# Attention with a mixture of experts: scaling and splitting v on GpSimd, and a softmax sum's constants by a two-tensor instruction

## The chip, the core and the metric

The kernel runs on one core of a Trainium2 chip. The metric is the time of one execution in device microseconds. TensorE (PE in the profile) does the matmuls, VectorE (DVE), ScalarE (ACT) and GpSimd (POOL) the element-wise work, and SyncE (SP) issues every DMA from one queue, in order. Each engine runs its own instructions in order and waits for others by semaphores.

## The reference, cut to what matters

```python
def _attn_ref(q, k, v, w1, b1, w2):          # q, k, v: 4 x 8 x 576 x 64
    scores = scale * np.matmul(q, k.transpose(0, 1, 3, 2))
    ...
    scores = scores + bias.transpose(2, 0, 1)[None, :, :, :]
    scores = scores - np.max(scores, axis=-1, keepdims=True)
    attn = np.exp(scores)
    attn = attn / (np.sum(attn, axis=-1, keepdims=True) + 1e-09)
    return np.matmul(attn, v).astype(np.float32)

def _moe_ref(x, w_gate, w1, w2):             # 2304 tokens, 8 experts
    P = np.exp(logits)
    ...
    for e in range(E):
        h = np.maximum(x @ w1[e], 0.0)
        ye = h @ w2[e]
        out += P[:, e:e + 1] * ye
```

The bias is a small network of the positions, the same in every batch. P is normalized by rows and columns eight times.

## The kernel before

All matmuls are done in float16. A float32 operand is scaled by a power of two and split into two float16 parts, hi (the rounded value) and lo (the rest), and products of the parts are summed. So a split is two instructions: one that scales and rounds, one that scales again and subtracts hi.

**The two parts of the program.** The first part, about 490 us long, is the attention, with the bias before it and the work of expert 0 mixed into it. The second part is experts 1 to 7. The change touches the first part alone.

**The attention.** There are 16 units: a batch and a pair of heads. Each unit has five steps: (gi 0, hh 0), (gi 0, hh 1), (gi 1, hh 0), (gi 1, hh 1) with two query tiles each, and gi 2 with one. Per unit, `u_load` fetches q and k, `u_cut` splits them into `qk` (ACT writes hi, DVE lo), and `u_trans` transposes `qk` on PE and has POOL copy rows of `qkT` between partitions. `u_vload` fetches v into `vnat`, of which there is one buffer; `u_v` splits it into `vs` with `asplit`: ACT writes `vs[:, 0]`, DVE `vs[:, 1]`. Three POOL copies (`pairs`) then arrange a third plane, `vs[:, 2]`, out of hi and lo. `vs` has two buffers (units 2 and 3 use room in `xb` instead). A tile of a step goes: scores on PE; `st_max` on DVE (a custom instruction, ISA in the listings, which adds the bias, writes `sb` and its extreme to `st`); `st_exp` on ACT, with the sums into `st`; `st_rcp` on DVE, two instructions on one or two columns of `st` (add 1e-9 and multiply by 2^-14, then the reciprocal); `st_hi` on ACT and `st_lo` on DVE, which write the split probabilities `ah` (one in three into room in `xc`); a DMA transpose of `ah` into `aT`; and two steps later `attend` on PE, `pv`<-`aT`,`vs`.

**Filling work.** When a batch is done, `e0_pieces` gives its matmuls through expert 0 to PE with the lowest priority. Their first layer is evacuated by `l1_out`: ACT into `ys`, then two POOL instructions, a cast and a subtraction, into `area`.

**The order of the work.** Everything is recorded as nodes of a `Plan` with an engine, an estimated cost (`Engine.cost`) and its dependencies, and `Plan.emit` puts all engines' instructions in order by list scheduling with these estimates. A node that changes engine or cost thus moves others too. All recorded instructions have the line of the recorder's call, L211, so rows are told apart by tiles.

The calls that bring v in come from the table of hooks, where step number 5u belongs to unit u:

```python
hook(f - 3, lambda u=u: [u_vload(u), u_v(u)])
...
hook(2, lambda: [b_scale(2), u_vload(0), u_v(0), u_load(3), u_cut(3), u_trans(3)])
```

Of the kernel before, what the change touches and what calls it, by code (L numbers as in the profile page):

```python
# [10 lines left out]
F32 = mybir.dt.float32  # L11
U32 = mybir.dt.uint32
AF = mybir.ActivationFunctionType
ALU = mybir.AluOpType
# [4 lines left out]
P = 128  # L19
# [8 lines left out]
EPS = 1e-9  # L28
T14 = 2.0**14
TM14 = 2.0**-14  # L30
# [7 lines left out]
MXP = 2  # L38
K_VEC = (1, 4, 7)
TM16 = 2.0**-16  # L40
TINY = 2.0**-100


# [228 lines left out]
def attention_sinkhorn_moe(ctx, tc, q, k, v, w1, b1, w2, wg, m1, m2, xm, xm4, xf, sel, out):  # L272
# [10 lines left out]
    nc = tc.nc  # L283
    plan = Plan()
    vec, act, pool, pe, sync = (
        Engine(plan, e, n)
        for e, n in ((nc.vector, "dve"), (nc.scalar, "act"), (nc.gpsimd, "pool"), (nc.tensor, "pe"), (nc.sync, "dma"))
    )

    consts = ctx.enter_context(tc.tile_pool(name="consts", bufs=1))  # L290
# [7 lines left out]
    def sm(shape):  # L298
        used[0] += shape[1]
        assert used[0] <= SMALL  # L300
        return sms[: shape[0], used[0] - shape[1] : used[0]]
# [5 lines left out]
    def bcast_max(psum_tile, mx, n, between=None):  # L307

        pt = psum_tile()
        pe.transpose(pt[:n, :P], mx, ident)  # L310
        col = sm([n, 1])
        vec.tensor_reduce(out=col, in_=pt[:n, :P], axis=AX.X, op=ALU.max)
        diag = sm([n, n])
        vec.tensor_scalar(out=diag, in0=ident[:n, :n], scalar1=col[:, 0:1], scalar2=None, op0=ALU.mult)
        if between is not None:
            between()
        pb = psum_tile()
        pe.matmul(pb[:, :n], ones[:n, :], diag, start=True, stop=True)
        res = sm([P, n])
        vec.tensor_copy(res, pb[:, :n])  # L320
        return res

    def pow2(mx, n, unit, clamp):

        p = sm([P, n])
        vec.tensor_single_scalar(out=p.bitcast(U32), in_=mx.bitcast(U32), scalar=0x7F800000, op=ALU.bitwise_and)
        u = sm([P, n])
        vec.tensor_scalar(out=u, in0=p, scalar1=clamp, scalar2=unit, op0=ALU.max, op1=ALU.mult)
        s = sm([P, n])
        vec.reciprocal(out=s, in_=u)  # L330
        return u, s

    def absmax(o, i):
        vec.tensor_reduce(out=o, in_=i, axis=AX.X, op=ALU.max, apply_absolute_value=True)
# [8 lines left out]
    def split(hi, lo, src, s):  # L343
        vec.tensor_scalar(out=hi, in0=src, scalar1=s, scalar2=None, op0=ALU.mult)
        vec.scalar_tensor_tensor(out=lo, in0=src, scalar=s, in1=hi, op0=ALU.mult, op1=ALU.subtract)

    def asplit(hi, lo, src, s):
        act.activation(hi, src, AF.Copy, scale=s)
        vec.scalar_tensor_tensor(out=lo, in0=src, scalar=s, in1=hi, op0=ALU.mult, op1=ALU.subtract)
# [15 lines left out]
    def xs(part, dt, pos, W):  # L365
        b, o = pos // 512, pos % 512
        return xv[b][:, part, dt, o : o + W]
# [47 lines left out]
    with ExitStack() as actx:  # L415
# [40 lines left out]

        make_identity(nc, ident)
        nc.gpsimd.memset(ones, 1.0)
        nc.vector.tensor_copy(id16, ident)


# [55 lines left out]
        absmax(mxb[:, 0:1], wb.rearrange("p a k -> p (a k)"))  # L517
        u_wb, s_wb = pow2(mxb[:, 0:1], 1, 2.0**-9, TINY)
        wbs = scon.tile([P, 2, 2, HID], F16, name="wbs")
# [4 lines left out]
        for kind in range(1, 4):  # L524
            vec.scalar_tensor_tensor(
                out=wr,
                in0=wbs[:, kind // 2, kind % 2, :],
                scalar=selt[:, kind : kind + 1],
                in1=wr,
                op0=ALU.mult,  # L530
                op1=ALU.add,
# [3 lines left out]
            out=wa.rearrange("p g (j k) -> p (g j) k", j=4),  # L535
            in0=wr.unsqueeze(1).broadcast_to([P, 16, HID]),
            in1=selt[:, 8:24].unsqueeze(2).broadcast_to([P, 16, HID]),
            op=ALU.mult,
# [89 lines left out]
        def bias_step(between=()):  # L628
# [22 lines left out]
        absmax(mxb[:, 1:2], w2b)  # L651
        u_w2, s_w2 = pow2(mxb[:, 1:2], 1, TM14, TINY)

        w1r = scon.tile([P, 2], F32, name="w1r")
        vec.tensor_scalar(
            out=w1r, in0=pw[:, H : H + 2], scalar1=s_wb[:, 0:1], scalar2=2.0**-11, op0=ALU.mult, op1=ALU.mult
# [5 lines left out]
            out=w2m,  # L662
            in0=w2r.unsqueeze(2).broadcast_to([P, H, 4]),
            in1=selt[:, 4:8].unsqueeze(1).broadcast_to([P, H, 4]),
            op=ALU.mult,
# [65 lines left out]
        def pairs(o, i):  # L731
            pool.tensor_copy(o.bitcast(U32), i.bitcast(U32))

        def u_v(u):
            if u >= len(units):
                return
            st = U[u]
            if u in (2, 3):
                o = 30 * D * (u - 2)
                vs = xb[:, o : o + 30 * D].rearrange("p (w h c d) -> p w h c d", w=3, h=2, c=5)  # L740
            else:
                vs = uni.tile([P, 3, 2, 5, D], F16, name="vs", tag="vs")
            vf = lambda t: t.rearrange("p h c d -> p (h c) d")
            asplit(vf(vs[:, 0]), vf(vs[:, 1]), vf(st.pop("vn")), vbox[1])

            pairs(vs[64:128, 2], vs[0:64, 0])
            pairs(vs[0:64, 2, :, 1:5], vs[64:128, 0, :, 0:4])
            pairs(vs[0:64, 2, :, 0], vs[0:64, 0, :, 4])
            st["vs"] = vs
# [59 lines left out]
        with plan.urgent():  # L809
# [6 lines left out]
            out=c8, in0=u_qk[:, 0:1], scalar=0.125, in1=u_qk[:, 1:2], op0=ALU.mult, op1=ALU.mult  # L816
# [7 lines left out]
            out=g, in0=g0, scalar=s_qk[:, 0:1], in1=s_qk[:, 1:2], op0=ALU.mult, op1=ALU.mult  # L824
# [11 lines left out]
        mv8, vbox = sm([P, 8]), []  # L836
# [6 lines left out]
        def v_scale():  # L843
            mv = sm([P, 1])
            vec.tensor_reduce(out=mv, in_=mv8, axis=AX.X, op=ALU.max)
            with plan.urgent():
                u_, s_ = pow2(bcast_max(ps_small, mv, 1), 1, TM14, TINY)
            vbox.extend((u_[:, 0:1], s_[:, 0:1]))
# [101 lines left out]

        def st_rcp(s):
            st, n = s["st"], len(s["ts"])
            vec.tensor_scalar(
                out=st[:, 3, :n], in0=st[:, 2, :n], scalar1=EPS, scalar2=TM14, op0=ALU.add, op1=ALU.mult
            )
            vec.reciprocal(out=st[:, 3, :n], in_=st[:, 3, :n])

# [29 lines left out]
        def attend(u, gi, ss):  # L987
# [25 lines left out]
            def fin():  # L1013
                hi, lo = xs(0, hp, pos, W), xs(1, hp, pos, W)
                act.activation(hi, ps[:, :W], AF.Copy, scale=TM16)
                vec.scalar_tensor_tensor(
                    out=lo, in0=ps[:, :W], scalar=TM16, in1=hi, op0=ALU.mult, op1=ALU.subtract
                )
# [29 lines left out]
        def w_scale(which):  # L1048
# [7 lines left out]
            with plan.urgent():  # L1056
                u_, s_ = pow2(bcast_max(ps_small, m, n), n, TM14, TINY)
            wsc[which] = (u_[:, 0:1], s_[:, 0:1])
# [88 lines left out]
        for n in range(NS + LAG + 1):  # L1147
            while xevac:
                xevac.pop(0)()
            if 0 < n <= NS:  # L1150
                st_rcp(steps[n - 1])
# [15 lines left out]
            if 0 < n <= NS:  # L1167
                s = steps[n - 1]
                st_hi(s)
                st_lo(s)  # L1170
                u, gi, hh = s["key"]
# [24 lines left out]
        vec, act, pool, pe, sync = nc.vector, nc.scalar, nc.gpsimd, nc.tensor, nc.sync  # L1196
# [289 lines left out]
    def w_max(e, w):  # L1486
# [20 lines left out]
        def scale(mx):  # L1507
# [3 lines left out]
            vec.tensor_single_scalar(out=p.bitcast(U32), in_=m.bitcast(U32), scalar=0x7F800000, op=ALU.bitwise_and)  # L1511
            vec.tensor_scalar(out=u, in0=p, scalar1=TINY, scalar2=TM12, op0=ALU.max, op1=ALU.mult)
            vec.reciprocal(out=s, in_=u)
# [487 lines left out]
```

## Time and profile before

| | us |
|---|---|
| median of 3 runs | 1741.65 (1737.5 to 1742.94) |
| the profiled execution | 1741.8 |
| its span, first to last instruction | 1740.0 |
| PE busy in the span | 1666.5 (96%) |
| DVE busy | 1437.2 (83%) |
| ACT busy | 1057.8 (61%) |
| POOL busy | 149.3 (9%) |

The span is what the trace shows; 1.8 us of the execution's own time lie outside of it. Busy shares are averages over the two parts, which have different limits, so the prediction reads the first part by itself.

### The profile page before, as it was taken

To read this page: it belongs to the slowest core of one execution; us is meant where nothing else is said; L and a number is where in the kernel's file an instruction comes from. 1 tells how busy PE (TensorE), PEld (TensorE's weight loads), DVE (VectorE), ACT (ScalarE), POOL (GpSimd) and SP (SyncE) were. 2 spreads that over 40 slices of the span, in tenths; PEclk is the share of its full clock that TensorE was granted. 3 is DMA by queue.
4 is the path that set the end of the run, shared out by engine and by line. 5 is a ranking of instruction groups with operands and counts; after the bars stand their busy time and mean duration, and the time that the engine had idled before them with its cause. 6 is when DMAs were issued, how large, how long until landed. Compare 5 with 4: busy or idle time off the path is not lost.

```text
span 1740.0 us, 40362 instructions
## 1 busy us (share of the span) xinstructions
PE 1666.5 (96%) x16596; PEld 1367.8 (79%) x16596; DVE 1437.2 (83%) x2595; ACT 1057.8 (61%) x1879; POOL 149.3 (9%) x191
## 2 busy tenths in 40 slices
PE   7887897999999999999999999999999999999998
PEld 4554564656585888888988898889888888888887
DVE  7998999889769999687878887988788878876666
ACT  7887888888857555456455545555555644443443
POOL 0102231323212300000000000000000000000000
PEclk9988898999999999999999999999999999999999
DMA  7869999999875446644664555456544743462321
GB/s 256 257 174 233 186 205 216 212 213 213 177 239 200 158 161 239 232 150 143 217 231 170 176 190 209 176 178 238 203 165 159 279 157 131 183 225 97 102 75 37
DMA packets 291964, 324.60 MB, mean 187 GB/s; under 512 B 183100, under 2 KB 217412, under 8 KB 286788
## 3 DMA queue, kind: packets, MB, share of 16 engines
q1 hardware_dynamic: 291780, 322.04, 61.6%
q8 instruction: 129, 2.11, 0.5%
q14 instruction: 55, 0.45, 0.1%
HBM read 191.43 MB, written 88.08 MB: 161 GB/s over the span
## 4 chain that ended last, share of the span: by engine, by line
PE 76%; DVE 5%; DMA 2%; ACT 1%; issue 1%; POOL 0%; DVEq 0%; SPq 0%; ACTq 0%; POOLq 0%
PE bankA L1612 18%; PE bankA L1632 14%; PE bankE L1632 9%; PE bankB L1632 9%; PE bankE L1612 9%; PE l L211 6%; PE bankB L1612 4%; PE pv L211 3%; PE s L211 2%; DMA aT<-ah 1%; PE bankB L375 1%; DVE c L1224 1%; DMA xb<-in_moe_w_dram 1%; PE bankE L375 1%; DVE ah L211 0%
## 5 line engine op out<-in xcount | busy, mean ns | idle before, releaser
L1612 PEld LDWEIGHTS <-slot 128*128 128x128 f16 x5040 | 451.0, 98 | 52.2 <-issue 6.4
L1632 PEld LDWEIGHTS <-hA 128*128 128x128 f16 x2268 | 221.0, 98 | 26.6 <-DVE hA L1224 1.2
L211 PEld LDWEIGHTS <-area 128*128 128x128 f16 (+1 forms) x2477 | 153.6, 100 | 101.3 <-issue 31.7
L1612 PE MATMUL bankA<-xt,slot 128*128 128x256 f16 (+1 forms) x1680 | 186.1, 262 | 1.4 <-ACT u L1669 1.4
L1612 PE MATMUL bankE<-xt,slot 128*128 128x256 f16 (+1 forms) x1680 | 186.1, 262 | 0.3 <-DVE c L1224 0.3
L1657 ACT ACTIVATE hA<-c 128x512 f16<-128x512 f32 x189 | 118.3, 628 | 107.8 <-DVE c L1224 106.8
L1632 PEld LDWEIGHTS <-hS 128*128 128x128 f16 x1512 | 147.6, 98 | 20.2 <-DVE hS L1663 1.9
L1632 PEld LDWEIGHTS <-area 128*128 128x128 f16 x1512 | 147.7, 98 | 17.1
L1716 ACT COPY u<-bankA 128x512 f32<-128x512 f32 (+1 forms) x70 | 38.0, 542 | 181.3 <-PE bankA L1632 181.2
L1224 DVE SCALAR_TENSOR_TENSOR hA<-c,hA 128x512 f16<-128x512 f32 x189 | 128.4, 691 | 15.9 <-ACT hA L1657 13.9
L1669 ACT ACTIVATE u<-bankA 128x512 f32<-128x512 f32 x126 | 75.2, 597 | 79.0 <-PE bankA L1612 72.2
L211 ACT ACTIVATE sb<-sb,st 128x576 f32<-128x576 f32 x144 | 110.5, 769 | 8.7 <-DVE st L211 8.5
L211 PE MATMUL l<-area 128*128 128x512 f16 (+1 forms) x413 | 110.6, 384 | 4.7 <-ACT area L211 1.3
L211 DVE SCALAR_TENSOR_TENSOR ah<-sb,st,ah 128x576 f16<-128x576 f32 x121 | 101.8, 869 | 13.4 <-ACT ah L211 12.9
L1224 DVE SCALAR_TENSOR_TENSOR acc<-c,fs,acc 128x256 f32<-128x256 f32 x252 | 110.3, 479 | 2.1
L211 ACT ACTIVATE ah<-sb,st 128x576 f16<-128x576 f32 x121 | 88.5, 770 | 19.3 <-DMA aT<-ah 14.4
L211 PE MATMUL s<-qkT 128*128 128x512 f16 (+3 forms) x560 | 82.7, 296 | 16.1 <-DVE st L211 14.7
L1632 PE MATMUL bankA<-area,hS 128*128 128x256 f16 x756 | 88.9, 273 | 1.8 <-ACT hS L1657 1.0
L1632 PE MATMUL bankA<-area,hA 128*128 128x256 f16 x756 | 88.4, 273 | 1.0 <-DVE hA L1224 1.0
L1632 PE MATMUL bankB<-area,hA 128*128 128x256 f16 x756 | 88.3, 273 | 0.0
L1632 PE MATMUL bankB<-area 128*128 128x256 f16 x756 | 88.3, 273 | 0.0
L1632 PE MATMUL bankA<-area 128*128 128x256 f16 x756 | 88.3, 273 | 0.0
(248 smaller groups left out, 3192.2 us busy)
## 6 DMA issues: line engine op xcount, KB each, us to landing
sc_w<-stage SPq DMA_DIRECT2D x84, 512.0 KB
acc<-sc_y SPq DMA_DIRECT2D x102, 256.0 KB
area<-sc_w SPq DMA_DIRECT2D x48, 512.0 KB
sc_y<-acc SPq DMA_DIRECT2D x84, 256.0 KB
xt<-sc_t SPq DMA_DIRECT2D x20, 1024.0 KB
slot<-sc_w SPq DMA_DIRECT2D x36, 512.0 KB
bt<-sc_bias SPq DMA_DIRECT2D x26, 576.0 KB
raw<-in_moe_w_dram SPq DMA_DIRECT2D x28, 512.0 KB
```

The lines of the kernel that those rows point to most:

```text
L211: self.plan.record(self.name, cost, lambda: fn(*args, **kw), ins, outs, move)
L375: pe.matmul(ps, w[:, a, ft * P : (ft + 1) * P], xs(xp, dt, p0, W), start=(dt == 0 and j == 0), stop=(dt == 3 and j == 2),)
L1224: vec.scalar_tensor_tensor(out=o, in0=x, scalar=s, in1=y, op0=op0, op1=op1)
L1612: pe.matmul(ps[:, jf * w : jf * w + w], t[:, a, c * 512 + f * P : c * 512 + f * P + P], x(xp, c), start=(first and jf == 0 and c == 0 and ...
L1632: pe.matmul(ps[:, j * 256 : j * 256 + 256], h[:, a, fc * w + j * P : fc * w + j * P + P], t[:, wp, fc * 256 : fc * 256 + 256], start=(firs ...
L1657: on_act(0.58, lambda: act.activation(h[:, 0, sl], x, AF.Relu if relu else AF.Copy), [r], wk)
L1669: on_act(0.55, lambda: act.activation(tmp[k], bank[b], f, scale=HS), [b], [k], 0)
L1716: on_act(0.27 * nt, lambda: act.copy(tmp[k][:, :n], bank[b][:, :n]), [b], [k], 0)
```

## The change

The first edit: a new helper `gsplit` does the split of v on POOL alone, in three instructions: scale `vnat` in place, copy it to hi (with a cast to float16), subtract hi from it into lo. `VG` has all 16 units, so `asplit` is not used for v any more. The second edit: in `st_rcp` the first instruction is a scalar_tensor_tensor that multiplies the sum by 2^-14 and adds a constant tile, `eps14`, of 1e-9 times 2^-14. Its inputs are two tensors in SBUF, where the old one had one tensor and two constants.

```diff
+VG = tuple(range(16))
...
+    def gsplit(hi, lo, src, s, on_act=False):
+        if on_act:
+            act.activation(hi, src, AF.Copy, scale=s)
+        pool.tensor_scalar(out=src, in0=src, scalar1=s, scalar2=1.0, op0=ALU.mult, op1=ALU.mult)
+        if not on_act:
+            pool.tensor_copy(hi, src)
+        pool.tensor_tensor(out=lo, in0=src, in1=hi, op=ALU.subtract)
...
+        eps14 = consts.tile([P, 2], F32, name="eps14")
+        nc.gpsimd.memset(eps14, EPS * TM14)
...
-            asplit(vf(vs[:, 0]), vf(vs[:, 1]), vf(st.pop("vn")), vbox[1])
+            (gsplit if u in VG else asplit)(vf(vs[:, 0]), vf(vs[:, 1]), vf(st.pop("vn")), vbox[1])
...
-            vec.tensor_scalar(
-                out=st[:, 3, :n], in0=st[:, 2, :n], scalar1=EPS, scalar2=TM14, op0=ALU.add, op1=ALU.mult
+            vec.scalar_tensor_tensor(
+                out=st[:, 3, :n], in0=st[:, 2, :n], scalar=TM14, in1=eps14[:, :n], op0=ALU.mult, op1=ALU.add
             )
```

The listings show the order of instructions on an engine, with the tile written, the tiles read and the shape. DVE and ACT have 16 instructions fewer, POOL has 48 more and one memset. First POOL, where expert 0's evacuations (`area`<-`ys`) begin beside units 4 and 5. Before:

```order
L211 COPY vs_145<-vs_145 64x2x32
L211 CAST area<-ys_108 128x512
L211 TENSOR_TENSOR area<-ys_108,area 128x512
L211 COPY qkT_127<-qkT_127 64x576 x2
L211 COPY qkT_129<-qkT_129 64x576 x2
L211 COPY vs_147<-vs_147 64x320
L211 COPY vs_147<-vs_147 64x2x128
L211 COPY vs_147<-vs_147 64x2x32
```

And with the change:

```order
L212 TENSOR_TENSOR area<-ys_110,area 128x512
L212 TENSOR_SCALAR vnat_118<-vnat_118,sms 128x640
L212 CAST area<-ys_110 128x512
L212 CAST vs_149<-vnat_118 128x640
L212 TENSOR_TENSOR area<-ys_110,area 128x512
L212 TENSOR_TENSOR vs_149<-vnat_118,vs_149 128x640
L212 CAST area<-ys_110 128x512
L212 COPY vs_149<-vs_149 64x320
L212 TENSOR_TENSOR area<-ys_110,area 128x512
L212 COPY qkT_129<-qkT_129 64x576 x2
```

The three instructions on v now stand between the evacuations, and a two-tensor one on v follows a two-tensor one on `ys`. On DVE, one step of unit 4's softmax. Before:

```order
L211 RECIPROCAL st_132<-st_132 128x2
L211 TENSOR_SCALAR st_135<-st_135 128x1
L211 SCALAR_TENSOR_TENSOR vs_145<-vnat_116,sms,vs_145 128x640
L211 SCALAR_TENSOR_TENSOR ah_142<-sb_136,st_146,ah_142 128x576
L211 SCALAR_TENSOR_TENSOR ah_142<-sb_137,st_146,ah_142 128x576
L211 SCALAR_TENSOR_TENSOR xa<-pv_112,xa 128x256
```

And with the change, about the same place:

```order
L212 SCALAR_TENSOR_TENSOR st_134<-st_134,eps_107 128x2
L212 ISA sb_136,st_141<-s_119,bt_124,sms 128x576
L212 ISA st_141 128x1
L212 SCALAR_TENSOR_TENSOR area<-area,sms 128x1024
L212 SCALAR_TENSOR_TENSOR ah_144<-sb_138,st_148,ah_144 128x576
L212 SCALAR_TENSOR_TENSOR ah_144<-sb_139,st_148,ah_144 128x576
L212 SCALAR_TENSOR_TENSOR xa<-pv_114,xa 128x256
L212 RECIPROCAL st_134<-st_134 128x2
```

The split of v is gone from the row ahead of `ah`, and the sum's instruction reads the new tile. On SP, with the change, where v of a later unit is fetched:

```order
L212 DMA_TRANSPOSE aT_0_120<-ah_144 128x9x128
L212 DMA vnat_118<-in_v_dram 64x2x320
L212 DMA_TRANSPOSE aT_127<-xc 128x18x128
L212 DMA vnat_118<-in_v_dram 64x2x256
L212 DMA bt_124<-sc_bias 128x1152
```

The fetch of v stands between two transposes, as before; what it waits for is the last reader of `vnat`, which was DVE's instruction and is now the third one of POOL.

## Rows read from the trace of the kernel before

**Rows 1.** Windows: stretch, length, busy PE, PEld, DVE, ACT, POOL, PE clock, DMA.

```profile
60.00:200.00 140.00, 113.25 (x1358) 70.04 (x1356) 130.43 (x276) 116.76 (x227) 19.98 (x36) 0.89 0.85 210
200.00:490.00 290.00, 269.53 (x2723) 173.95 (x2719) 249.09 (x556) 235.25 (x479) 86.53 (x109) 0.98 0.99 205
...
490.00:1740.00 1250.00, 1235.29 (x11860) 1094.12 (x11859) 1010.44 (x1680) 661.45 (x1090) 40.96 (x36) 1.00 0.50 176
```

**Rows 2.** PE's waits from 60 to 490 us: total us, times, longest.

```profile
PE s L211 <- DVE st L211: 17.9, 18, 3.0
PE l L211 <- DVE qk L211: 7.3, 4, 2.8
PE pv L211 <- DMA aT<-ah: 4.2, 5, 1.9
```

**Rows 3.** The tile vs: count, ns min/median/max, first and last start.

```profile
L211 ACT ACTIVATE vs<-vnat,sms x14: 816/824/859, 104.8 to 449.5; 128x640 f16<-128x640 f32 x14
L211 DVE SCALAR_TENSOR_TENSOR vs<-vnat,sms,vs x14: 866/1047/1133, 105.8 to 450.6; 128x640 f16<-128x640 f32 x14
```

**Rows 4.** DVE's groups by form, 60 to 490 us: count, busy us, mean ns, idle before.

```profile
L211 DVE SCALAR_TENSOR_TENSOR ah<-sb,st,ah 128x576 f16<-128x576 f32 x121 | 101.8, 869 | 13.4 <-ACT ah L211 12.9 <-issue 0.3
...
L211 DVE SCALAR_TENSOR_TENSOR qk<-nat,sms,qk 128x576 f16<-128x576 f32 x32 | 26.7, 862 | 0.2 <-ACT qk L211 0.2
L211 DVE SCALAR_TENSOR_TENSOR xc<-sb,st,xc 128x576 f16<-128x576 f32 x23 | 20.3, 919 | 1.4 <-ACT xc L211 1.4
L211 DVE TENSOR_SCALAR st<-st 128x2 f32<-128x2 f32 x64 | 17.2, 269 | 1.3 <-ACT sb L211 1.3
L211 DVE SCALAR_TENSOR_TENSOR vs<-vnat,sms,vs 128x640 f16<-128x640 f32 x14 | 14.0, 999 | 0.0
L211 DVE RECIPROCAL st<-st 128x2 f32<-128x2 f32 x64 | 10.3, 162 | 1.3
...
L211 DVE SCALAR_TENSOR_TENSOR xa<-pv,xa 128x64 f16<-128x64 f32 x15 | 3.2, 213 | 0.1
```

**Rows 5.** The tile st: count, ns min/median/max.

```profile
L211 DVE SCALAR_TENSOR_TENSOR ah<-sb,st,ah x121: 791/812/1719, 88.3 to 482.5; 128x576 f16<-128x576 f32 x121
L211 DVE TENSOR_SCALAR st<-st x80: 131/160/1162, 79.5 to 473.5; 128x2 f32<-128x2 f32 x64, 128x1 f32<-128x1 f32 x16
```

**Rows 6.** POOL's groups by form, 60 to 490 us.

```profile
L211 POOL TENSOR_TENSOR area<-ys,area 128x512 f16<-128x512 f32 x26 | 33.0, 1269 | 2.1
```

**Rows 7.** POOL's forms in the tile ys, and line 1796 of the second part.

```profile
L211 POOL CAST area<-ys x27: 608/611/1263, 199.7 to 490.9; 128x512 f16<-128x512 f32 x27
L211 POOL TENSOR_TENSOR area<-ys,area x27: 1156/1162/1712, 201.1 to 491.6; 128x512 f16<-128x512 f32 x27
...
L1796 POOL TENSOR_SCALAR acc<-acc,fs x18: 694/1264/2273, 575.1 to 698.3; 128x512 f32<-128x512 f32 x18
```

**Rows 8.** Timeline near 200, 251 and 329.9 us: start, length, engine, instruction.

```profile
199.66 0.87 DVE L211 SCALAR_TENSOR_TENSOR vs<-vnat,sms,vs 128x640 f16<-128x640 f32 x1
...
200.56 1.29 SPq L211 DMA_DIRECT2D vnat<-in_v_dram  x2
200.70 2.55 DVE L211 SCALAR_TENSOR_TENSOR ah<-sb,st,ah 128x576 f16<-128x576 f32 x2 [0.16 <-ACT ah L211]
...
201.09 1.54 POOL L211 TENSOR_TENSOR area<-ys,area 128x512 f16<-128x512 f32 x1
...
251.13 1.16 POOL L211 TENSOR_TENSOR area<-ys,area 128x512 f16<-128x512 f32 x1
...
251.76 0.42 DVE L211 SCALAR_TENSOR_TENSOR xb<-pv,xb 128x256 f16<-128x256 f32 x1 [0.97 <-ACT xb L211]
...
329.90 1.16 POOL L211 TENSOR_TENSOR area<-ys,area 128x512 f16<-128x512 f32 x1
329.92 1.16 DVE L211 TENSOR_SCALAR st<-st 128x2 f32<-128x2 f32 x1
```

## The prediction

> **What bounds the kernel now.** I read the windows first, because the busy shares of the whole span mix two parts. From 490 us on the change has no instruction, and PE is busy 1235 of 1250 us [rows 1]: whatever happens before can only move that part as a block. In the attention there are two stretches. From 60 to 200 us DVE is the busiest, 130.4 of 140 us, ahead of ACT with 116.8 and PE with 113.3. From 200 to 490 us, where expert 0's matmuls fill PE's gaps, PE is the busiest, 269.5 of 290 us, and DVE has 249.1 [rows 1]. The next view is PE's waits: its longest ones in the attention are for DVE, 17.9 us for the extremes in `st` before the next scores and 7.3 us for `qk` [rows 2]. So DVE's time counts in full in the first stretch, and in the second only as far as PE waits for it. POOL is busy 20.0 and 86.5 us there [rows 1]: it has room.
>
> Then I looked at how long equal instructions take, since POOL gets more work. DVE's `ah` instruction, with both tensors in SBUF, has a median of 812 ns and a longest of 1719 [rows 5], and the timeline shows why: two of them take 2.55 us instead of 1.62 while a POOL two-tensor instruction runs from 201.09 to 202.63 [rows 8]. The sum's TENSOR_SCALAR on two columns, median 160 ns [rows 5], takes 1.16 us from 329.92 on, as long as the POOL instruction that began 0.02 us earlier [rows 8]. An instruction that reads one tensor from PSUM goes through beside POOL with its 0.42 us [rows 8], and the reciprocal, one small tensor, has a mean of 162 ns [rows 4]. So some DVE instructions stand still while POOL works, and the change gives POOL more such work.
>
> **The change, part by part.** *Removed.* DVE loses 16 splits at 0.999 us (the mean of the 14 in `vs`, the two in `xb` taken like them), 16.0 us [rows 4]; ACT loses 16 at 0.824 us, 13.2 us [rows 3].
>
> *Added on POOL.* The form on 512 columns gives the length on 640 by 640/512: the cast 0.611 us becomes 0.76, the two-tensor one 1.162 becomes 1.45, and the scaling, 0.694 at its shortest in line 1796, becomes 0.87 [rows 7]. That is 3.08 us a unit and 49.3 us in all. I take the shortest for the scaling, since its median of 1.264 us there holds waits; with the median it would be 1.58. POOL's 106.5 busy us in these 430 us become about 156, so POOL doesn't become the bound. The chain on v grows from two instructions to three, but v is fetched and split some steps before its unit's `attend`, so I cost that at nothing; if that cover is gone, a unit pays up to 3.08 − 0.82 = 2.3 us.
>
> *What POOL takes from DVE.* Now, DVE loses to POOL: on `ah` 121 × (869 − 812) = 6.9 us, on the same shape in `xc` 23 × (919 − 812) = 2.5, on `qk` 32 × (862 − 812) = 1.6, on the sums 64 × (269 − 160) = 7.0 [rows 4, 5]; 18.0 us together. Spread over all of POOL's 106.5 us [rows 1] that is 0.17 us per POOL us, and the new 49.3 us would cost 8.3 us. Charged to the 26 two-tensor instructions alone, 33.0 us [rows 6], it is 0.55 per us, and the new two-tensor work, 16 × 1.45 = 23.2 us, costs 12.6 us. I take 12.6, because the large stretches in the rows stand beside two-tensor instructions [rows 8]. The ends: nothing, if the new work falls where DVE reads PSUM; and 16 × (0.91 + 0.17 × 1.63) = 19.0 us, if every new two-tensor one costs as much as the longest `ah` shows, 1.719 − 0.812 = 0.91 us [rows 5], and the other two the average rate.
>
> *The sums.* 80 TENSOR_SCALAR become two-tensor instructions on one or two columns. No row shows one so small beside POOL. The nearest in kind, `ah` and `qk`, stand still beside POOL [rows 4, 5, 8], so I take it that the new one does too: same length, same waits, nothing gained. The ends: 7.0 us gained if it never waits, and 80 × 0.05 = 4 us lost if it is as long as the split of 64 columns, 213 ns against 160 [rows 4, 5].
>
> The Trainium skill, page "SBUF — State Buffer", section "Who interferes with whom", states that a VectorE instruction with two SBUF inputs contends with a GpSimd one that reads SBUF, that one in a two-port mode contends with any, and that whichever comes second blocks for the other's whole instruction. By this rule the sums win nothing, as I take it; by the reading that only the old form waits, the 7.0 us would go. Taken to its end, with DVE always arriving just behind POOL, the rule would make all 49.3 us of new POOL work a loss, 1741.8 + 20.8 = 1762.6 by the shares used below; the trace shows one sixth of POOL's time lost [rows 1, 4], so I don't forecast that and leave it a chance of 0.03.
>
> *The sum.* DVE: −16.0 + 12.6 = −3.4 us. Four of the 16 units lie in the first stretch (the fifth is split at its end, at 199.66 [rows 8]) and count in full, −0.85; twelve lie in the second, −2.55, of which I count half, because PE's waits there are mostly for DVE [rows 2] while PE is otherwise full: −1.3. ACT's 13.2 us I count at nothing: it is not the busiest in either stretch [rows 1], and DVE's work covers it; if that cover went, ACT's relief would be gain on top. SP: the next fetch of v went out 0.03 us behind DVE's last reading of `vnat` at 200.53 (`vs` on DVE, 0.87 us from 199.66 on) [rows 8] and now follows POOL's third instruction; the planner has put it in its place in SP's queue, so nothing, with the rival below as the price. The memset of `eps14` is one of several at the start, in which nobody waits: nothing. In all −2.1 us: 1741.8 − 2.1 = 1739.7 us. The profiled execution, 1741.8, is 0.15 us from the median of the runs, so I make no correction.
>
> **The rivals.** *The sums are freed.* The small two-tensor instruction is not held by POOL. Then the 7.0 us go, and with them the sums' part of the new loss, 7.0/18.0 of 12.6 = 4.9 us: DVE has 15.3 us less, 3.8 in full and 11.5 by half, −9.6: 1732.2 us. For it: the reciprocal, as small, never waits [rows 4]. Against: every two-tensor form from SBUF that I have a row of does [rows 4, 5].
>
> *The new POOL work falls in gaps.* Nothing is added, DVE has 16.0 us less, 4.0 in full and 12.0 by half, −10.0: 1731.8 us. For it: DVE spends much time on instructions that read PSUM and pass POOL [rows 8]. Against: 18.0 us are lost with two thirds of the POOL work already.
>
> *SP is held up, slower.* The fetch of v stands between transposes, and it waits for POOL's third instruction, which is behind in the queue of POOL and is itself stretched by DVE (1.54 against 1.16 us [rows 7, 8]). If it comes later than planned, the transposes behind it start later, and `pv` on PE waits, as it does now 5 times for 4.2 us in all [rows 2]. At 1.0 us for each of the twelve units of the second stretch, passed on in full, that is +12.0 − 2.1 = +9.9: 1751.7 us. It decides against the change from (5.2 + 2.1)/12 = 0.61 us a unit. For it: PE is full there, so lost time is not regained. Against: between the fetch and the split lie several transposes, and the next fetch isn't urgent for some steps.
>
> **How the numbers follow.** A measurement can tell about 0.3%, 5.2 us, from no change. My forecast, with its small change either way, 0.42; the sums freed 0.23; the gaps 0.12; SP held up 0.20; every POOL instruction a loss 0.03. Both faster rivals lie beyond 1736.4, the slower ones beyond 1746.9, so faster 0.35, same 0.42, slower 0.23. The bounds of the unknown costs give 1741.8 − 14.4 = 1727.4 (DVE less by 16.0 + 7.0 = 23.0, a quarter in full, the rest by half) and 1741.8 + 4.4 = 1746.2 (DVE more by 3.0 + 4.0 = 7.0, in the same shares). The range from 1730 to 1750 takes in both faster rivals and leaves out a part of the slower cases and the outermost low end, about 2 in 10.
>
> **What would show it.** Right: `ah`'s mean goes up from 869 ns and the mean of the sums' instruction stays well over 200; POOL's busy time in the attention goes to about 156 us or, with its own waits, somewhat over; DVE's busy time there falls by a few us only; PE's waits for DVE keep their size; the second part keeps its length. Wrong: the sums' instruction at a mean near 160 ns; or PE's waits for `aT` at 10 us and more; or an attention that ends over 5 us earlier or later.

## The result, and the profile after

The changed kernel takes **1748.54 us** (median of 6 runs, 1745.13 to 1751.24), the kernel before 1739.74 (6 runs on the same chip, 1737.50 to 1742.94). The ratio is 1.0051, 95% interval 1.0040 to 1.0062: slower by 8.8 us, where 1739.7 was forecast. The profiled execution of the change took 1751.19 us with a span of 1749.4, so it is one of the longer of its six; that of before took 1741.8.

Where the attention ends is read from the router's matmuls into `bankS`, the first instructions of the second part. The tile view of `bankS` (duration ns min/median/max, then first and last start), before and, in the second fence, after:

```profile
L1280 PE MATMUL bankS<-wgs,xa x72: 166/166/214, 490.8 to 501.5; 128*128 128x8 f16 x72
```

```profile
L1291 PE MATMUL bankS<-wgs,xa x72: 166/166/214, 500.9 to 511.5; 128*128 128x8 f16 x72
```

The attention ends at 500.9 instead of 490.8 us. From there to the end it is 1749.4 − 500.9 = 1248.5 us, before 1740.0 − 490.8 = 1249.2. So the whole difference lies in the attention, as the prediction had it, with the other sign. Windows of after, with the columns of [rows 1] (the mean granted clock is the third number from the end):

```profile
60.00:200.00 140.00, 112.59 (x1374) 70.11 (x1374) 130.88 (x269) 113.74 (x222) 38.51 (x50) 0.90 0.84 210
200.00:490.00 290.00, 262.92 (x2609) 167.16 (x2608) 250.13 (x545) 225.97 (x464) 124.64 (x138) 0.96 0.97 195
200.00:500.00 300.00, 272.73 (x2708) 175.30 (x2706) 251.59 (x547) 228.32 (x468) 127.01 (x142) 0.97 0.98 197
500.00:1749.00 1249.00, 1235.13 (x11861) 1094.18 (x11859) 1010.53 (x1680) 660.90 (x1090) 41.34 (x37) 1.00 0.50 176
```

Against [rows 1]: DVE is no less busy (130.88 and 250.13 for 130.43 and 249.09), although it has 16 instructions of 1 us fewer. Up to the end of its attention ACT has 342.1 us (113.74 + 228.32), before 352.0, and POOL has 165.5 for 106.5. The second stretch has grown from 290 to 300 us, and PE's share of that is 27.3 us idle (300 − 272.7) for 20.5 before, and 3.2 us more busy time for the same work at a granted clock of 0.96 to 0.97 for 0.98.

DVE's groups by form, 60 to 500 us, as in [rows 4] (count, busy us, mean ns, idle before):

```profile
L212 DVE SCALAR_TENSOR_TENSOR ah<-sb,st,ah 128x576 f16<-128x576 f32 x121 | 109.4, 928 | 13.4 <-ACT ah L212 13.3
L212 DVE SCALAR_TENSOR_TENSOR qk<-nat,sms,qk 128x576 f16<-128x576 f32 x32 | 31.8, 1008 | 1.1 <-ACT qk L212 1.1
L212 DVE SCALAR_TENSOR_TENSOR xc<-sb,st,xc 128x576 f16<-128x576 f32 x23 | 20.9, 936 | 1.3 <-ACT xc L212 1.3
L212 DVE SCALAR_TENSOR_TENSOR st<-st,eps 128x2 f32<-128x2 f32 x64 | 18.1, 283 | 0.4 <-ACT sb L212 0.4
...
L212 DVE SCALAR_TENSOR_TENSOR st<-st,eps 128x1 f32<-128x1 f32 x16 | 5.4, 338 | 1.6 <-ACT sb L212 1.6
```

By the prediction's own rule (mean less undisturbed length, times count) DVE now loses to POOL 14.0 us on `ah`, 2.9 on `xc`, 6.3 on `qk`, 7.9 on the sums of two columns, and on those of one column, which before had a mean of 146 ns, 16 × (338 − 146) = 3.1: **34.2 us for 18.0**. The timeline shows one of the new sums standing still, DVE first, then POOL (start, length):

```profile
390.87 0.17 DVE L212 RECIPROCAL st<-st 128x2 f32<-128x2 f32 x1
390.95 1.37 DVE L212 SCALAR_TENSOR_TENSOR st<-st,eps 128x1 f32<-128x1 f32 x1
...
390.90 1.40 POOL L212 TENSOR_TENSOR vs<-vnat,vs 128x640 f16<-128x640 f32 x1
```

An instruction on one element per lane takes 1.37 us, from 0.05 us behind the start of POOL's to 0.02 behind its end.

PE's waits, 60 to 500 us (total, times, longest), against [rows 2]:

```profile
PE s L212 <- DVE st L212: 23.6, 27, 2.1
PE pv L212 <- DMA aT<-ah: 6.0, 5, 2.3
PE l L212 <- DVE qk L212: 4.3, 3, 2.3
...
PE pv L212 <- DMA aT<-xc: 3.4, 2, 2.5
```

The wait for `st` has grown by 5.7 us, those for `aT` from 4.2 to 9.4, and that for `qk` has shrunk by 3. SyncE's own waits for POOL, the mark of the rival in which SP is held up, are small (60 to 500 us):

```profile
SPq L212 <- POOL xb L212: 1.6, 1, 1.6
SPq L212 <- POOL vs L212: 0.7, 2, 0.4
```

What goes with a pause of PE shows in two ten-microsecond windows of after (PE waits 2.52 us for `aT` before 354.55):

```profile
350.00:360.00 10.00, 6.67 (x64) 4.29 (x63) 5.37 (x10) 6.66 (x13) 0.30 (x1) 0.83 1.22 225
360.00:370.00 10.00, 9.90 (x121) 7.68 (x118) 9.15 (x19) 7.93 (x18) 6.27 (x7) 1.00 0.73 133
```

The granted clock of the first slice is 0.83, so a part of it ran at 1.2 GHz, where the next slice has 2.4 GHz throughout.

### The profile page after: what moved, and what is told of

It is laid out like the page before. It is cut to its first block, busy times and chain, and to the rows that moved or that the text cites. A ratio compares the mean times of both kernels' runs of the same rounds, so it can differ in the third digit from the quotient of the medians.

```text
span 1749.4 us, 40374 instructions
## 1 busy us (share of the span) xinstructions
PE 1668.6 (95%) x16596; PEld 1369.2 (78%) x16596; DVE 1440.4 (82%) x2579; ACT 1047.2 (60%) x1863; POOL 208.7 (12%) x240
## 4 chain that ended last, share of the span: by engine, by line
PE 72%; DVE 6%; DMA 3%; ACT 1%; issue 1%; POOL 0%; DVEq 0%; ACTq 0%; SPq 0%; POOLq 0%
PE bankA L1623 18%; PE bankA L1643 14%; PE bankE L1643 9%; PE bankB L1643 9%; PE bankE L1623 9%; PE bankB L1623 5%; PE l L212 3%; PE pv L212 2%; DMA aT<-ah 2%; PE s L212 1%; PE bankB L384 1%; DMA aT<-xc 1%; DVE ah L212 1%; DVE sb L212 1%; PE bankE L384 1%
## 5 line engine op out<-in xcount | busy, mean ns | idle before, releaser
L212 DVE SCALAR_TENSOR_TENSOR ah<-sb,st,ah 128x576 f16<-128x576 f32 x121 | 109.4, 928 | 13.4 <-ACT ah L212 13.3
```

Source lines behind the costliest of these rows:

```text
L212: self.plan.record(self.name, cost, lambda: fn(*args, **kw), ins, outs, move)
```

## The experiments

The two edits do four things: they take work off DVE and ACT, put work on POOL, give the sums another form, and move instructions on all engines, since the planner sees other costs. The experiments separate these. "Old order" means that the planner was told the costs of ACT and DVE for v, so that PE and SP have the same instructions in the same order as before; "new order" means that it was told POOL's. "Attention" is the start of the first `bankS` matmul in the one profiled execution, and medians weigh more than it, because the runs of one kernel differ by 3 us and more. e1 to e4 and e13 to e16 ran on one chip, e5 to e8 on a second, e9 to e12 on a third; the ratio is to runs of the kernel before beside them.

| run | order | v is split by | sums | median us (runs) | ratio to before [95%] | attention |
|---|---|---|---|---|---|---|
| e1 | old | ACT, DVE | new | 1741.18 (11) | 1.0006 [0.9996, 1.0016] | 492.5 |
| e2 | new | POOL | old | 1746.04 (5) | 1.0033 [1.0020, 1.0046] | 496.4 |
| e3 | old | POOL | new | 1743.91 (7) | 1.0027 [1.0016, 1.0037] | 496.2 |
| e4 | new | ACT, DVE | new | 1754.58 (6) | 1.0081 [1.0068, 1.0095] | 506.3 |
| e5 | old | nobody | new | 1740.73 (12) | 1.0003 [0.9993, 1.0013] | 486.7 |
| e6 | old | ACT, DVE; POOL does as much besides | new | 1751.42 (6) | 1.0065 [1.0053, 1.0077] | 501.0 |
| e7 | new | nobody | new | 1743.50 (12) | 1.0021 [1.0013, 1.0029] | 492.5 |
| e8 | a third | ACT, DVE | new | 1745.74 (9) | 1.0030 [1.0020, 1.0040] | 493.7 |
| e9 | old | ACT, DVE in units 0 to 3, then nobody | new | 1744.31 (9) | 1.0028 [1.0019, 1.0038] | 493.7 |
| e10 | old | ACT, DVE; POOL does two of e6's three | new | 1744.56 (7) | 1.0029 [1.0019, 1.0040] | 495.3 |
| e11 | old | ACT, DVE | on ACT | 1738.72 (11, one of them 3442.57) | 0.9997 [0.9988, 1.0006] | 488.1 |
| e12 | a fourth | POOL | new | 1749.24 (6) | 1.0059 [1.0040, 1.0078] | 502.7 |
| e13 | old | POOL in units 0 to 3, then ACT, DVE | new | 1740.54 (12) | 1.0002 [0.9993, 1.0012] | 495.0 |
| e14 | old | nobody in units 0 to 3, then ACT, DVE | new | 1742.72 (11) | 1.0014 [1.0005, 1.0023] | 489.4 |
| e15 | as e9, once more | as e9 | new | 1741.29 (12) | 1.0012 [1.0001, 1.0023] | 495.6 |
| e16 | old | POOL in units 0 to 3, then ACT, DVE | on ACT | 1738.90 (11) | 0.9994 [0.9984, 1.0005] | 486.5 |

e9 and e15 are one kernel on two chips: 3 us apart, and as far in the ratio to the runs of before beside them. So a difference of 3 us between runs on different chips is not read as one here.

**Each edit alone, and both in the old order (e1, e2, e3).** For e1:

```diff
-VG = tuple(range(16))
+VG = ()
```

> The second edit alone; v is split by ACT and DVE, and every engine's order is that of the kernel before. If the sums' small instruction is held by POOL like the old form: within 2 us of the kernel before (1739.7 us), its mean on two columns near 269 ns, and the one-column form, which had no long ones before, now with a few (up to +3 us in all on DVE). If the new form were freed: mean near 155 ns, 7.0 us less on DVE, 1733 to 1736 us.

For e2 the sum's instruction is the old one, and the rest is as in the change:

```diff
-            vec.scalar_tensor_tensor(
-                out=st[:, 3, :n], in0=st[:, 2, :n], scalar=TM14, in1=eps14[:, :n], op0=ALU.mult, op1=ALU.add
+            vec.tensor_scalar(
+                out=st[:, 3, :n], in0=st[:, 2, :n], scalar1=EPS, scalar2=TM14, op0=ALU.add, op1=ALU.mult
```

> The first edit alone, in exactly the order of the changed kernel. If the whole loss is in the move of v (by port or by order): 1746 to 1750 us, as the changed kernel. If the sums' new form carries a part of it (the one-column form stood still 3.0 us more there): 1744 to 1746 us.

For e3 the three POOL instructions are recorded as nodes of ACT and DVE (`front` is POOL's scaling and cast, `back` its subtraction):

```diff
...
+        plan.record("act", act.cost("activation", hi, [src, s]), front, [src, s], [hi])
+        plan.record("dve", vec.cost("scalar_tensor_tensor", lo, [src, s, hi]), back, [src, s, hi], [lo])
```

> Both edits, but the planner is told that v is split on ACT and DVE at their costs, so PE, SP and all else stand in the order of the kernel before and POOL does the work at those places. Port theory (DVE standing still behind POOL's new instructions is the loss): 1747 to 1750 us, DVE's loss to POOL near 36 us as in the changed kernel. Order theory (the new order of SP and PE is the loss, three stalls of PE by late transposes and bias loads): 1737 to 1741 us.

The new form of the sums alone changes nothing that can be told (1.0006, with 1 inside the interval). It is not freed from POOL either. DVE's groups of e1, 60 to 500 us,

```profile
L212 DVE SCALAR_TENSOR_TENSOR st<-st,eps 128x2 f32<-128x2 f32 x64 | 15.2, 237 | 1.5 <-ACT sb L212 1.5
...
L212 DVE SCALAR_TENSOR_TENSOR st<-st,eps 128x1 f32<-128x1 f32 x16 | 4.4, 276 | 1.0 <-ACT sb L212 1.0
```

and the one-column form in the kernel before, 60 to 490 us:

```profile
L211 DVE TENSOR_SCALAR st<-st 128x1 f32<-128x1 f32 x16 | 2.3, 146 | 1.0 <-ACT sb L211 1.0
```

The sums of two columns went from 269 [rows 4] to 237 ns, those of one column from 146 to 276: 15.2 + 4.4 = 19.6 us, where the two forms had 17.2 + 2.3 = 19.5 before. e2, the change without the new sums, is 2.5 us under the change, with overlapping intervals. e3, both edits in the old order, is 2.7 us behind e1 on the same chip and, by ratio, ahead of the change (1.0027 against 1.0051, intervals apart). By this comparison about half of the loss is the order.

**The order alone (e4, e7, e5).** e4 has the change's order and before's work on v: the nodes are POOL's, the instructions ACT's (`front`) and DVE's (`back`).

```diff
...
+        plan.record("pool", pool.cost("tensor_scalar", src, [src, s]), lambda: None, [src, s], [src])
+        plan.record("pool", pool.cost("tensor_copy", hi, [src]), front, [src, s], [hi])
+        plan.record("pool", pool.cost("tensor_tensor", lo, [src, hi]), back, [src, s, hi], [lo])
```

> The order of the changed kernel, but v is split by ACT and DVE at the places where POOL's second and third instruction stood; the sums in the new form. Port theory: DVE loses to POOL near 18 us as before, 1739 to 1743 us. Order theory: 1746 to 1752 us, PE idle near 27 us from 200 to 490 us as in the changed kernel.

e5 and e7 leave the split of v out, in the old and in the new order; the buffers are cleared once, so that v is zero:

```diff
...
+        def front():
+            if first:
+                g.memset(hi, 0.0)
...
+        def back():
+            if first:
+                g.memset(lo, 0.0)
```

> The order of the kernel before, the sums' new form, and v not split at all (the buffers of the first four units are cleared once; the products with v are left out of account), so DVE has 16.0 us and ACT 13.2 us less and POOL nothing more. If removed DVE time is worth what the prediction counted (a quarter in full, the rest by half): 10 us under e1's 1741.2, about 1731 us. If v's split lay in slack: 1737 to 1740 us, and then the loss of e3 (1743.9) is mostly what POOL takes from DVE at dear places.

> As e5, in the order of the changed kernel: against e5 it shows that order alone. Order theory: 4 to 6 us over e5. If the new order is only slow together with POOL's work: within 2 us of e5.

These three carry the main reading. In the **old** order all of v's split, 16 us of DVE and 13 of ACT, can go, and the time stays (e5 1.0003 against e1 1.0006; e5's profile is its fastest run, so its early end at 486.7 says less than its median). In the **new** order the same work is worth 11.1 us (e4 1754.58 less e7 1743.50, on two chips): the planner had counted none of it on ACT and DVE there. Whether it is missing room that costs so much was not looked into. And without any work on v the new order is behind the old one by 2.8 us on the same chip (e7 against e5). From e7 to the change it is 5.0 us for POOL's work.

**POOL's work alone (e6, e10).** Order and work on v of before, and POOL does in addition the same three instructions on constants; they write the third plane of `vs`, which thereby is partly wrong. e10 leaves the last line out.

```diff
...
+            g.tensor_scalar(out=z3, in0=one, scalar1=s, scalar2=1.0, op0=ALU.mult, op1=ALU.mult)
+            g.tensor_copy(z3, one)
...
+            g.tensor_tensor(out=z3, in0=one, in1=z3, op=ALU.subtract)
```

> The order of the kernel before, v split on ACT and DVE, and in addition POOL does three instructions of the same kind and length on constants, written into the third plane of vs (whose values are so not those of the reference). It takes nothing off DVE and adds the standing still alone. If that costs what DVE's sum says: DVE's loss 12 to 16 us up, 1741.2 + 6 to 8 us by the prediction's shares, 1747 to 1749 us. If standing still costs nothing where PE is full: 1741 to 1743 us. With e5, the two parts should add up: e3 minus e5 about e6 minus e1.

> Order of the kernel before, v split by ACT and DVE, and POOL does in addition, per unit, a scaling and a cast of constants into a plane of vs that nobody reads (in an earlier run these two and a subtraction cost 10.2 us: 1751.4 against 1741.2). Theory A, DVE stands still in proportion to POOL's time: about two thirds of POOL's added time stays, so 6 to 7 us: 1747 to 1748. Theory B, the instruction with two tensors carries the loss (it reads twice as much): 1742 to 1744. Theory C, the casts and scalings alone carry it: 1750 to 1752.

e6 is 10.2 us behind e1, on two chips. Waits of ACT and of PE in e6, 60 to 500 us:

```profile
ACT ys L212 <- POOL area L212: 6.2, 6, 2.7
...
PE s L212 <- DVE st L212: 20.7, 24, 2.4
PE l L212 <- DVE qk L212: 10.0, 4, 4.2
```

PE's waits for DVE's `st` and `qk` are 30.7 us together, in e1 23.2, and PE waits 1.2 us for POOL itself, in e1 0.7. But POOL is also later with expert 0's evacuations, and ACT waits for it before it writes `ys` again: 6.2 us here, 0.8 in e10, no such row in e1. How much of the 10.2 us goes this way, and not over DVE, was not tried. DVE's groups of e6, 60 to 500 us, and behind them those of e10:

```profile
L212 DVE SCALAR_TENSOR_TENSOR ah<-sb,st,ah 128x576 f16<-128x576 f32 x121 | 108.1, 919 | 11.5 <-ACT ah L212 11.2 <-issue 0.3
...
L212 DVE SCALAR_TENSOR_TENSOR st<-st,eps 128x2 f32<-128x2 f32 x64 | 19.2, 300 | 1.5 <-ACT sb L212 1.5
L361 DVE SCALAR_TENSOR_TENSOR vs<-vnat,sms,vs 128x640 f16<-128x640 f32 x14 | 16.2, 1154 | 0.0
```

```profile
L212 DVE SCALAR_TENSOR_TENSOR ah<-sb,st,ah 128x576 f16<-128x576 f32 x121 | 106.2, 905 | 11.3 <-ACT ah L212 10.8 <-issue 0.3
...
L361 DVE SCALAR_TENSOR_TENSOR vs<-vnat,sms,vs 128x640 f16<-128x640 f32 x14 | 17.0, 1215 | 0.0
L212 DVE SCALAR_TENSOR_TENSOR st<-st,eps 128x2 f32<-128x2 f32 x64 | 15.7, 245 | 1.3 <-ACT sb L212 1.3
```

By the same rule over all forms (`qk`, `xc` and the one-column sums stand in rows not shown), with `vs` against its 999 ns, DVE loses 32.6 us in e6 and 25.2 in e10, against 18.2 in e1. POOL's added time comes from the windows of e1, of e6 and of e10 (POOL is the fifth busy time):

```profile
60.00:200.00 140.00, 114.85 (x1371) 70.89 (x1367) 130.95 (x276) 118.03 (x228) 19.44 (x36) 0.88 0.86 211
...
200.00:500.00 300.00, 278.96 (x2941) 181.01 (x2940) 256.28 (x568) 238.60 (x485) 87.52 (x111) 0.97 0.99 207
```

```profile
60.00:200.00 140.00, 113.83 (x1354) 70.32 (x1352) 131.91 (x271) 116.87 (x225) 39.05 (x50) 0.88 0.83 208
...
200.00:500.00 300.00, 272.74 (x2726) 174.74 (x2724) 264.39 (x561) 236.43 (x481) 132.29 (x142) 0.97 0.96 199
```

```profile
60.00:200.00 140.00, 114.37 (x1355) 71.39 (x1354) 130.70 (x273) 117.06 (x226) 30.66 (x45) 0.88 0.83 209
...
200.00:500.00 300.00, 276.98 (x2858) 178.68 (x2858) 261.17 (x567) 237.81 (x483) 111.98 (x133) 0.97 0.97 205
```

It is 171.3 − 107.0 = 64 us in e6 and 142.6 − 107.0 = 36 in e10. So a scaling or a cast costs DVE 7.0/36 = 0.20 us per POOL us, the two-tensor instruction (32.6 − 25.2)/(64 − 36) = 0.26: **DVE's loss goes by POOL's time**, not by the two-tensor instructions alone. In time e10 costs a third of e6 (+3.4 of +10.2, on two chips), between theories A and B and nearer to B: what is shown for DVE's loss is not shown for the time.

**What the removed work was worth (e9, e15, e14).** For e9 and e15 the split stays in units 0 to 3, and the later ones read what units 0 and 1 left (their v is left out); e14 leaves out the first four alone, their planes cleared.

```diff
...
+        nv[0] += 1
+        first = nv[0] <= 4
...
+            if first:
+                sc.activation(hi, src, AF.Copy, scale=s)
...
```

> Order of the kernel before, sums in the new form. The v of units 0 to 3 is split by ACT and DVE as before; the v of units 4 to 15 is not split at all, so 12 x 1.0 us of DVE and 12 x 0.82 us of ACT are gone from the stretch 200 to 490 us, and those units' heads read what units 0 and 1 left there (this part of the computation is left out). The prediction's share (one half of what DVE is spared in that stretch): 6 us under the same kernel with its v split (1741.2), so 1735. Theory that v's split lies in slack there, because its result is wanted some 20 us later and the path that sets the end runs through q, k, a and the sums: 1739.5 to 1742.

> The same kernel as the one whose units 4 to 15 have no split of v (1744.3; the v of those units is left out). Its profile lost 3.1 us before the first softmax, where it has no instruction that differs, and nothing from there to the end of the attention. If that early loss is an accident of single executions: a second profile without it, and 1740 to 1742 in the median. If it belongs to this kernel as loaded: the same loss again, 1743 to 1745.

> As the run before, but the v of units 0 to 3 is not split at all (their planes are cleared by POOL, so these units' part of the output is left out as zero). DVE is spared 4 x 1.0 us and ACT 4 x 0.82 us in the first stretch, where DVE is the busiest engine. If the prediction's full count holds there: 1737.2 (1741.2 - 4.0). If the split is slack there as it was from unit 4 on: 1740 to 1742.

On the chip of e1 (1741.18) e15 gave 1741.29 and e14 1742.72, on another e9 gave 1744.31: **no part of the removed work shows**, where the prediction's shares ask for 6 and 4 us. Where DVE's time went instead: its waits from 200 to 495 us in e1, and in e9.

```profile
DVE ah L212 <- ACT ah L212: 12.8, 13, 2.6
DVE sb L212 <- PE s L212: 9.9, 11, 1.9
DVE xc L212 <- ACT xc L212: 6.8, 5, 4.6
DVE xb L212 <- ACT xb L212: 3.3, 3, 1.4
```

```profile
DVE ah L212 <- ACT ah L212: 16.4, 13, 3.5
DVE sb L212 <- PE s L212: 14.1, 13, 2.7
DVE xc L212 <- ACT xc L212: 7.2, 4, 4.8
DVE xb L212 <- ACT xb L212: 4.3, 3, 2.4
```

These four grew by 9.2 us, and DVE's busy time from 200 us to the end of the attention fell by 9.6 (249.1 to 239.5). What DVE no longer did, it waited: for ACT's half of `ah` and for PE's scores. PE's wait for `st` in the same window was 9.2 us in e1 and 8.9 in e9. e9's profile also lost 3.1 us before the first softmax's reciprocal, with a granted clock of 0.83 from 50 to 60 us (1.00 in e1); e15's lost 2.3 there. Nothing that the kernels differ in has run by then; what sets it is open.

**Other orders (e8, e12).** e8 is e1's work with the planner told 0.7 us for DVE's half of v in place of 0.89; e12 is the change with the planner told POOL's measured lengths:

```diff
...
-        plan.record("dve", vec.cost("scalar_tensor_tensor", lo, [src, s, hi]), back, [src, s, hi], [lo])
+        plan.record("dve", 0.7, back, [src, s, hi], [lo])
```

```diff
...
+        plan.record("pool", 0.8, scale, [src, s], [src])
+        plan.record("pool", 0.99, top, [src], [hi])
+        plan.record("pool", 1.4, rest, [src, hi], [lo])
```

> The work of e1 (v on ACT and DVE, the sums' new form), with a third order: the planner is told 0.7 us instead of 0.89 for DVE's half of the split of v. If any new order near this one costs about as much as the changed kernel's: 1744 to 1748 us. If orders near this one are alike and the changed kernel's is bad for a reason of its own: 1739 to 1743 us.

> Both edits, the planner told POOL's measured lengths of the three instructions (0.80, 0.99 and 1.40 us), which gives an order that is neither that of the kernel before nor that of the change. Theory that the change's loss over the old order (1748.5 against 1743.9) is one draw among nearby orders: anything from 1743 to 1752. Theory that an order made with the true lengths is as good as the old one: 1741 to 1744. Theory that the work on POOL costs it whatever the order: 1748 to 1750.

A third order of unchanged work costs 4.6 us (e8 against e1, on two chips; the ratios' intervals are apart), and true lengths on POOL give an order no better than the change's. In three comparisons with equal work (e8, e7, and the change against e3) the old order came out ahead by 2.8 to 4.6 us, and in a fourth, e4 against e1, by 13.4: there the new order does work that it was not made for. One wait goes with the new order, DVE's for the load of the bias tile `bt`. In the change and, in the second fence, in e7, 60 to 500 us:

```profile
DVE sb L212 <- DMA bt<-sc_bias: 3.8, 2, 3.1
```

```profile
DVE sb L212 <- DMA bt<-sc_bias: 2.9, 2, 2.4
```

e2 and e4 have it too (3.4 and 3.2 us), and no run in the old order has it. In the change SyncE issues the load at 351.38, behind a transpose that stands in its queue from 346.80 on, and DVE stands until 356.43. e8's order has no such wait and loses all the same, so it is not the whole of what an order can lose, and what it costs by itself was not isolated.

**Versions that might beat both (e11, e13, e16).** The sums' factor on ACT, without the 1e-9; v on POOL only beside the first stretch, where expert 0 leaves POOL free; and both.

```diff
+            o, x = st[:, 3, :n], st[:, 2, :n]
+            plan.record("dve", 0.08, lambda: nc.scalar.activation(o, x, AF.Copy, scale=TM14), [x], [o])
```

> Work and order of the kernel before, but the scaling of a step's sums by 2^-14 is done by ACT instead of DVE; the addition of 1e-9 is left out. DVE is spared 80 x 0.15 us and the 7 us that these stood still behind POOL; on the chain of the sums comes the way from DVE to ACT and back. If the sums' standing still is on the path that sets the end (the prediction's rival of the freed sums): 1732 to 1737. If the way over ACT costs what the standing still did: 1738 to 1742. If it costs more, 16 steps x two waits of some 0.2 us: 1743 to 1748.

> Order of the kernel before, sums in the new form. Only units 0 to 3 have their v scaled and split by POOL, beside whose first stretch (60 to 200 us) stands none of expert 0's work on POOL; units 4 to 15 by ACT and DVE as before. The prediction counted the 4 us that DVE is spared there in full, and the new POOL work's loss is a quarter of the 15 us measured, 3.8: so -4.0 + 3.8, as good as the same kernel with v on ACT and DVE (1741.2): 1740 to 1742. Theory that DVE's time there is the limit and POOL's new work falls in gaps: 1737 to 1739. Theory that the split is slack there too and the loss is not: 1742 to 1745.

> Order of the kernel before, units 0 to 3 with v on POOL, and the sums' scaling by 2^-14 on ACT in place of DVE (the addition of 1e-9 is left out). The sums on ACT alone gave 1738.7, 1.0 under the kernel before and 2.5 under the new sums. If the two effects add up and the first four units on POOL cost nothing: 1738 to 1739; if they win their 4 us: 1734 to 1736; if they cost: 1740 to 1743.

None is faster than before beyond its interval (0.9997, 1.0002, 0.9994). With the sums on ACT, DVE is spared the 19.5 us of the sums, of which the standing still is 7, and the time is the same. What e11 pays in return is in its tile `st`: each of ACT's instructions takes 196 ns in the median, and DVE waits 11.4 us for them (in the list of who waited). So what freed sums would be worth by themselves is bounded by this only together with that price, and stays open.

```profile
L954 ACT ACTIVATE st<-st x80: 187/196/282, 79.1 to 472.4; 128x2 f32<-128x2 f32 x64, 128x1 f32<-128x1 f32 x16
...
  DVE st L211: 11.4, 15
```

## Why the prediction was wrong

**The step that failed** is the weighing of DVE's time: "Four of the 16 units lie in the first stretch ... and count in full", and "twelve lie in the second ... of which I count half, because PE's waits there are mostly for DVE". For the removed 16.0 us these shares make −10.0 us; in the old order e5 (−0.5 against e1), e14 (+1.5) and the two runs of e9's kernel (+3.1, +0.1) show no gain. The shares come from how busy DVE is and for whom PE waits, but not from who waits for v. The trace of before would have told. The tile `vs` there, who waited for it (us, times), and its first instructions:

```profile
L211 PE MATMUL pv<-aT,vs x1176: 189/272/422, 132.9 to 490.7; 128*64 128x256 f16 x138, 128*64 128x64 f16 x44, 64*64 64x64 f16 x13, 64*64 64x256 f16 x1
...
L211 DVE SCALAR_TENSOR_TENSOR vs<-vnat,sms,vs x14: 866/1047/1133, 105.8 to 450.6; 128x640 f16<-128x640 f32 x14
...
  POOL vs L211: 85.0, 13
...
  PEld L211: 0.2, 1
```

DVE writes the first `vs` at 105.8 us, PE reads it first at 132.9. In the whole attention PE waits 0.2 us for it. POOL waits 85.0, all of it for ACT's half, and that does not reach PE, whose waits from 60 to 490 us have no row for POOL. The extremes in `st`, for which PE waited 17.9 us [rows 2], come from another instruction. v's split stood in gaps that the chain of scores, extremes, exponentials and `ah` leaves on DVE, and without it DVE stands in the same gaps.

This holds for the old order. Taken the other way round, the new order first (e4 against e1, +13.4) and v's split off then (e7 against e4, −11.1), the two steps come to +2.3, as they do in the first way, where the prediction has −10.0. How these 2.3 us divide between order and removed work depends on the way.

**What POOL takes from DVE** was right in kind and too small: 12.6 us were taken, 34.2 − 18.0 = 16.2 came, inside the ends of 0 and 19.0. POOL's added time was 165.5 − 106.5 = 59.0 us for 49.3, and the choice to charge the two-tensor instructions alone is refuted by e10. Here the shares come nearer: they turn e6's added 14.4 us into 9.0, where 10.2 were measured, ACT's waits for POOL among them, and e10's 7.0 into 4.4, where 3.4 were. A stretched `ah`, `qk` or sum is on the chain, a split of v in the old order is not: **a microsecond taken off DVE and one put on it do not weigh the same.** Where v's split is gone, part of the added time may fall in the room it left: e3 is only 3.2 us behind e5, for 10.9 us of added standing still (30.5 less 19.6 by the same rule).

**The order** was priced only as SP held up. That rival's price was near the result (1751.7), but its mechanism is not what was seen: SyncE waited 2.3 us for POOL's writes to v in the whole attention, though PE's waits for `aT` did grow to 9.4, and e7 has the new order's loss without POOL's three instructions. The order itself was counted at nothing and costs 2.8 us (e7 against e5) to 4.6 (the change against e3).

**The sums**: right, nothing gained, and the new form stands still as the nearest rows did. That the one-column form, never long before, would now be held too was missed: 2.1 us in e1, which the two-column form gave back there, and 3.1 in the change. By the Trainium skill, page "SBUF — State Buffer", section "Who interferes with whom", a VectorE instruction with two SBUF inputs contends with a GpSimd one that reads SBUF, and the second blocks; the trace agrees, with the 1.37 us above.

From before to the change in four steps by medians: new sums +1.2 (not distinguishable from nothing), v's split off DVE and ACT −0.5, the new order +2.8, POOL's work in that order +5.0; together 8.5, measured 8.8. The steps cross chips, so each is good to some 2 or 3 us. The forecast's terms for the same steps were 0, −10.0, 0 and +7.9. Of the prediction's signs, the means of `ah` (928 ns) and of the sums (283) and POOL's busy time (165.5 us) came out as for a right one; an attention that ends 10.1 us later, and a DVE that is no less busy, did not.

## What to carry to other kernels

Before an instruction's time is counted as gain, look at who waits for its output, not at how busy its engine is: e5 took 16 us off DVE, the busiest engine of the first stretch and the one PE waits for most, and moved nothing. Time that another engine adds on the chain has to be counted as a loss: of each microsecond that DVE stood still longer, 0.7 us came out in e6 and 0.5 in e10, and 0.3 where v's split was gone (e3 against e5). When a list scheduler sets the order, change the costs it sees and the instructions apart from each other, as e3, e4 and e7 do; an order that comes out by itself can cost as much as the edit.

## What was not expected of the hardware

The sum's TENSOR_SCALAR on one column was never held by POOL (131 to 154 ns, though 4 of the 16 begin while POOL is in an instruction), on two columns it was (up to 1162 ns [rows 5]); as a two-tensor instruction it is held on one column as well, 276 ns in the mean of e1. POOL's scaling and cast, with one tensor each, hold DVE almost as much per microsecond (0.20) as its two-tensor instruction (0.26), by one trace each. POOL is slowed in turn: the cast to `vs` has a median of 988 ns and a shortest of 715 in the change. The 6 casts of 715 to 721 ns begin beside no DVE instruction with two tensors in SBUF; of the 8 of 949 to 1337 ns, 7 begin while DVE is in `ah` or `xc`.

```profile
L212 POOL TENSOR_SCALAR vnat<-vnat,sms x16: 797/798/1447, 103.6 to 461.3; 128x640 f32<-128x640 f32 x16
L212 POOL CAST vs<-vnat x14: 715/988/1337, 104.9 to 463.4; 128x640 f16<-128x640 f32 x14
L212 POOL TENSOR_TENSOR vs<-vnat,vs x14: 1389/1401/1917, 105.7 to 465.2; 128x640 f16<-128x640 f32 x14
```
